# Feature maps and v copies of later batches tied behind named instructions, and the first load of q in two halves, in a linear-attention and Fourier-gate kernel on one core

## The chip, the cores and the metric

The kernel runs on one core of one Trainium2 chip. The metric is the device time of one execution in microseconds (us). Before the change three runs gave 295.21, 295.63 and 296.19 us; their median is 295.63 us. One more execution was profiled, and everything read from a trace here is that execution.

Engine names are those of the profile: PE is TensorE (matrix multiply; PEld its weight loads), DVE is VectorE, ACT is ScalarE, POOL is GpSimd, SP is SyncE. Each engine takes its instructions in the order in which they stand in its own program.

## The reference, cut to what matters

Eight batches, 8 heads, 576 positions, 64 values per head. Each batch goes through a linear attention with cosine and sine feature maps, and the result through a gated long convolution done with Fourier transforms.

```python
def phi(x, c, s):                      # feature map, 64 -> 128
    r = np.maximum(x, 0.0)
    return np.concatenate([r * c, r * s], axis=-1)
q_p = phi(q, cos_w, sin_w)
k_p = phi(k, cos_w, sin_w)
kv  = einsum('bhsf,bhsd->bhfd', k_p, v)
z   = k_p.sum(axis=2)
att = einsum('bhsf,bhfd->bhsd', q_p, kv) / (einsum('bhsf,bhf->bhs', q_p, z) + 1e-6)
x    = att as [batch, 576, 512]
x1, x2, x3 = split(x @ w_proj, 3)
conv = irfft(rfft(x2) * rfft(filter))  # along the 576 positions
out  = (x1 * conv * x3) @ w_out
```

## The kernel before, in words

Everything of one batch runs in a chain of stages, and stages of neighbouring batches are woven into each other.

**Stages of a batch.** `load_qk`, `load_v`: DMAs issued by POOL bring q, k and v in fp16 into tiles named qraw, kraw, vraw; all of them share one ring of four buffers (line 104, 109), so a load waits until the readers of the tile four loads earlier are done. `emit_phi`: twelve DVE multiplications per tensor make the feature maps qp and kp. `emit_va`: four ACT copies per batch (line 116) bring v into va, where a column of ones already stands. `emit_qt`: PE transposes qp in four pieces qt, and DVE and ACT each copy half of a piece to qpt. `emit_kv`: 48 matmuls of kp with va, one ACT cast to kvs. `emit_num`: matmuls of qpt with kvs, then on DVE rcp (the divisor) and att (the quotient), four pieces. `emit_fx`: att through a small first Fourier factor, ACT casts to fx. `emit_x2`: the x2 projection in three pieces, ACT casts to x2f. `emit_dft`: the forward transform, ACT casts to xf, DVE multiplies by the filter's spectrum h3 (m, yf). `emit_gate`: x1 and x3 projections, ACT cast to x1s, DVE product g. `emit_inv`: the inverse transform, ACT casts to eo, DVE sums to y. `emit_out`: y times w_out, ACT scales to os, SP's DMAs store it.

**Order.** The code at the end of the kernel (lines 619 to 709) emits the stages in a chosen sequence, but a scheduler decides where each instruction stands on its engine: as long as its operands are expected to be there in time, it may stand far ahead of where it was written. That is why, before the change, copies of v2 stand among batch 0's instructions on ACT.

**First part, batches 0 to 2 (to about 107 us).** Besides the stages, tables are computed here: POOL makes index rows (`emit_iotas`), DVE and ACT make sines and cosines. The inverse tables (`emit_inv_tables`) go DVE tn_inv, then two POOL instructions on tg_a (lines 245, 248), then ACT iim and ire. `emit_h` makes the spectrum: POOL forms feo, PE h_ps and h_nyq, ACT casts to h3 (lines 392, 399), DVE copies h3 once more.

**Later batches.** One turn of the loop at line 673 interleaves, for b from 1: x2(b) with num(b+1), dft(b), gate(b) with fx(b+1), inv(b), then out(b-1) with qt(b+2), then kv(b+2). A turn ends about where the first tile of out starts on PE.

**PSUM.** All matmul results use one pool of four tiles ("u", line 63). A new result waits until the readers of the tile whose place it takes are done. In a turn the places go: inv tiles 0 to 3; out_0 takes inv_0's place, qt_0 inv_1's, out_2 inv_2's, qt_1 inv_3's; out_4 takes out_0's (so it waits for the first os on ACT), qt_2 takes qt_0's, qt_3 takes out_2's (second os), kv takes qt_1's (its qpt copy on ACT), and the third x2 tile takes the place of the second num tile (its att on DVE).

Of the kernel before, what the change touches and what calls it, by code (L numbers as in the profile page):

```python
# [2 lines left out]

# [14 lines left out]
def kernel(  # L18
# [83 lines left out]
    def load_qk(b, nm):
        src = q if nm == "q" else k
        rw = work.tile([NP, NH, NJ * D], FP16, tag="raw", bufs=4, name=f"{nm}raw{b}")
        raw_t[(b, nm)] = rw
        nc.gpsimd.dma_start(out=rw, in_=src[b].rearrange("h (p j) d -> p h (j d)", j=NJ))
# [294 lines left out]

    kp_t, qp_t, kvs_t, att_t, fx_t, xt_t = {}, {}, {}, {}, {}, {}

    def emit_phi(b, nm):
# [3 lines left out]
        for j in range(NJ):  # L408
            for cs, col in ((0, ccol), (1, scol)):
                tsc(  # L410
                    t[:, j, :, cs], rw[:, :, ds(j * D, D)],
                    col[0:NP, j : j + 1], AL.mult, 0.0, AL.max,
                )
# [14 lines left out]
    def emit_qt(b, hp):  # L428
        qp, qpt = qp_t[b], qpt_buf[0]
        u = psum.tile([128, 2, 1024], FP16, tag="u", bufs=4, name=f"qt{b}_{hp}")  # L430
        for hh in range(2):
            for j in range(NJ):
                nc.tensor.transpose(  # L433
                    u[:, hh, ds(j * NP, NP)],
                    qp[:, j, 2 * hp + hh].rearrange("p a b -> p (a b)"),
                    perm,
                )
        hsl = slice(2 * hp, 2 * hp + 2)
        nc.vector.tensor_copy(  # L439
            out=qpt[:, hsl, :, 0, 0:60],  # L440
            in_=u[:, :, 0:300].rearrange("p h (t c) -> p h t c", c=60),
        )
        nc.scalar.copy(  # L443
            out=qpt[:, hsl, ::-1, 1, 4:64],
            in_=u[:, :, 276:576].rearrange("p h (t c) -> p h t c", c=60),
        )

    def emit_num(b, hp):
        qpt, kvs = qpt_buf[0], kvs_t[b]
        if hp == 0:  # L450
            att_t[b] = work.tile([128, NT, DM], FP16, tag="att", bufs=2, name=f"att{b}")
        att = att_t[b]
        u = unit(f"num{b}_{hp}")
        for hh in range(2):
            h = 2 * hp + hh
            for t in range(NT):
                nc.tensor.matmul(
                    u[:, hh, ds(t * 65, 65)], qpt[:, h, t].rearrange("p a b -> p (a b)"),
                    kvs[:, h // 4, ds((h % 4) * 65, 65)], start=True, stop=True,
                )  # L460
# [4 lines left out]
        nc.vector.tensor_tensor(  # L465
            out=att[:, :, ds(hp * 128, 128)].rearrange("p t (h d) -> p h t d", h=2),
            in0=nv[:, :, :, 0:D],
            in1=rcp.unsqueeze(3).to_broadcast([128, 2, NT, D]),
            op=AL.mult,
        )  # L470

    def emit_fx(b, cs=range(NC)):
        att = att_t[b]
        if 0 in cs:
            fx_t[b] = work.tile([128, NC, 24, 48], FP16, tag="fx", bufs=2, name=f"fx{b}")
        fx = fx_t[b]
        for c in cs:
            u = unit(f"fx{b}_{c}")
# [17 lines left out]
        nc.scalar.copy(  # L496
            out=fx[:, :, :, 40:48],
            in_=cu.rearrange("p u (c r) -> p (u c) r", c=2)[:, :, 0:192].rearrange(
                "p c (g o) -> p c g o", o=8
            ),  # L500
        )
# [4 lines left out]
    def emit_x2(b, bls=range(3)):  # L506
        fx = fx_t[b]
        if 0 in bls:
            moe.setdefault(b, {})["x2f"] = work.tile([NP, 3, 2, DM], FP16, tag="x2f", name=f"x2f{b}")
        x2f = moe[b]["x2f"]  # L510
        for bl in bls:
            u = unit(f"x2_{b}_{bl}")
            for comp in range(2):
                for c in range(NC):
                    nc.tensor.matmul(  # L515
                        u[0:NP, comp],
                        fx[:, c, ds(comp * 6 + 2 * bl, 2)].rearrange("p a b -> p (a b)"),
                        wp16[:, c, ds(DM, DM)], start=(c == 0), stop=(c == NC - 1),
                    )
            nc.scalar.mul(out=x2f[:, bl], in_=u[0:NP], mul=X2SC)  # L520

    def emit_dft(b):
        x2f = moe[b]["x2f"]
        yf = work.tile([NP, 3, 2, DM], FP16, tag="yf", name=f"yf{b}")
        moe[b]["yf"] = yf
        for bl in range(3):
            u = unit(f"dft{b}_{bl}")
            for comp, tab in ((0, tre), (1, tim)):
                nc.tensor.matmul(u[0:NP, comp], tab[:, bl], x2f[:, bl, comp], start=True, stop=True)  # L529
            xf = work.tile([NP, 2, DM], FP16, tag="xf", bufs=2, name=f"xf{b}_{bl}")  # L530
            nc.scalar.copy(out=xf, in_=u[0:NP])  # L531
            m1 = work.tile([NP, 2, DM], FP16, tag="m1", bufs=1, name=f"m1_{b}_{bl}")
            m2 = work.tile([NP, 2, DM], FP16, tag="m2", bufs=1, name=f"m2_{b}_{bl}")
            nc.vector.tensor_tensor(out=m1, in0=xf, in1=h3[:, bl, 1:3], op=AL.mult)  # L534
            nc.vector.tensor_tensor(
                out=m2, in0=xf, in1=h3[:, bl, 0].unsqueeze(1).to_broadcast([NP, 2, DM]), op=AL.mult
            )
            nc.vector.tensor_tensor(out=yf[:, bl, 0], in0=m1[:, 0], in1=m2[:, 1], op=AL.subtract)  # L538
            nc.vector.tensor_tensor(out=yf[:, bl, 1], in0=m1[:, 1], in1=m2[:, 0], op=AL.add)

    def emit_gate(b, c):
# [16 lines left out]
        nc.scalar.copy(out=x1s, in_=us[0][:, :, 0:HS])  # L558
        for hf in range(2):
            nc.vector.tensor_tensor(  # L560
                out=(g[:, c, 0:HS] if hf == 0 else g[:, c, HS:S][:, ::-1]).rearrange(
                    "p (j i o) -> p j i o", j=3, i=6
                ),
# [176 lines left out]
```

## Time and profile before

| what | value |
|---|---|
| three runs, median (lowest to highest) | 295.63 us (295.21 to 296.19) |
| the profiled execution's own time | 295.97 us |
| its span, first to last instruction | 294.2 us |
| mean granted TensorE clock | 0.949 |
| busy ACT, DVE, POOL | 198.5, 211.0, 40.2 us |
| issue of the first q load (576 KB) to its landing | 6.12 us |
| busy PE in 34 to 84 us, and in 107.1 to 136.7 us | 38.42 of 50 us, 28.86 of 29.6 us |

A line of the timeline reads: start and duration in us, engine, line of the code, operation, output<-input, shapes, how many were merged, and in square brackets how long the engine stood idle before it and what ended that wait. The chain of waits lists, in order of time, the pieces of work that follow from each other up to the last instruction.

### The profile page before, as it was taken

How to read it: one execution, taken by the hardware profiler on the slowest of the kernel's cores; microseconds unless marked ns; L12 is line 12 of the kernel's file. 1: busy time of each engine (PE TensorE's matmuls, PEld its weight loads, DVE VectorE, ACT ScalarE, POOL GpSimd, SP SyncE). 2: the span in 40 equal slices, each digit the busy share in tenths (PEclk: the TensorE clock that was granted, in tenths of full speed). 3: DMA queues.
4: the chain of work that ended last, by engine and by line, in shares of the span. 5: the costliest groups of instructions: out<-in, count | busy, mean ns of one | idle time of the engine just before them, and what ended most of it. 6: DMA issues, size and time to landing. Idle time of an engine off the chain costs nothing.

```text
span 294.2 us, 6029 instructions
## 1 busy us (share of the span) xinstructions
PE 255.1 (87%) x2379; PEld 179.8 (61%) x2379; DVE 211.0 (72%) x678; ACT 198.5 (67%) x266; POOL 40.2 (14%) x47
## 2 busy tenths in 40 slices
PE   0667883797899999899989998999999999999960
PEld 0554652744485867587758775877587768657620
DVE  4989498569699966996699669965796279508700
ACT  2186472969877779677967796776577767665531
POOL 8420839420102100300020000000000000000000
PEclk9999898579689999999999999999999999999995
DMA  7999889469235906690569050005000500050055
GB/s 95 204 205 207 139 125 196 60 89 178 21 63 78 166 2 163 88 156 0 164 84 159 1 163 2 0 3 163 0 0 2 162 1 2 0 160 3 1 162 160
DMA packets 26941, 26.67 MB, mean 91 GB/s; under 512 B 1632, under 2 KB 22112, under 8 KB 26912
## 3 DMA queue, kind: packets, MB, share of 16 engines
q0 software_dynamic: 21152, 16.84, 38.6%
q1 hardware_dynamic: 5760, 9.44, 11.6%
q8 instruction: 18, 0.29, 0.4%
q14 instruction: 11, 0.09, 0.1%
HBM read 33.69 MB, written 9.44 MB: 147 GB/s over the span
## 4 chain that ended last, share of the span: by engine, by line
PE 55%; DVE 17%; DMA 10%; ACT 7%; issue 4%; POOL 3%; SPq 1%; ACTq 0%; POOLq 0%; DVEq 0%
PE x L552 19%; PE out L601 9%; PE inv L578 9%; DMA vraw<-in_v_dram 7%; PE x L515 7%; DVE kp L90 7%; PE qt L433 5%; PE fx L480 3%; DVE qp L90 3%; DVE att L465 3%; ACT x2f L520 2%; POOL tg_a L245 2%; DMA qraw<-in_q_dram 2%; PE dft L529 1%; ACT va L116 1%
## 5 line engine op out<-in xcount | busy, mean ns | idle before, releaser
L552 PE MATMUL x<-fx,wp 128*128 128x288 f16 x512 | 69.0, 290 | 3.1 <-ACT fx L496 1.5
L552 PEld LDWEIGHTS <-wp 128*128 128x128 f16 x512 | 50.6, 99 | 17.7 <-issue 2.9
L515 PE MATMUL x<-wp,fx 128*96 128x512 f16 x192 | 45.1, 381 | 2.1 <-DVE att L465 1.7
L484 ACT CAST fx<-fx 128x960 f16<-128x960 f32 x32 | 30.3, 960 | 14.7 <-PE fx L480 14.6
L433 PE MATMUL qt<-perm,qp 96*128 96x96 f16 x384 | 24.2, 224 | 16.0 <-DVE qp L90 9.8
L520 ACT ACTIVATE x2f<-x 96x1024 f16<-96x1024 f32 x24 | 24.5, 1022 | 19.4 <-PE x L515 19.4
L116 ACT COPY va<-vraw 96x768 f16<-96x768 f16 x32 | 26.0, 836 | 16.9 <-DMA vraw<-in_v_dram 16.9
L601 PE MATMUL out<-wo,y 128*128 128x512 f16 x160 | 37.3, 379 | 0.0
L433 PEld LDWEIGHTS <-qp 96*128 96x128 f16 x384 | 21.8, 108 | 21.2 <-DVE qp L90 10.9
L560 DVE TENSOR_TENSOR g<-x,x1s 128x288 f16<-128x288 f32 x64 | 27.1, 447 | 9.3 <-PE x L552 5.0
L515 PEld LDWEIGHTS <-fx 128*96 128x96 f16 x192 | 22.2, 123 | 17.2 <-DVE att L465 2.5
L605 ACT ACTIVATE os<-out 128x1024 f32<-128x1024 f32 (+1 forms) x24 | 20.8, 882 | 15.7 <-PE out L601 10.9
L439 DVE COPY qpt<-qt 128x600 f16<-128x600 f16 x32 | 14.8, 467 | 17.0 <-PE qt L433 16.5
L465 DVE TENSOR_TENSOR att<-num,rcp 128x640 f16<-128x640 f32 x32 | 26.0, 819 | 0.2
L534 DVE TENSOR_TENSOR m<-xf,h 96x1024 f16<-96x1024 f16 x24 | 16.4, 682 | 13.4 <-ACT xf L531 13.2
L601 PEld LDWEIGHTS <-y 128*128 128x128 f16 x160 | 15.1, 98 | 15.3
L578 PEld LDWEIGHTS <-yf 96*128 96x128 f16 x192 | 19.3, 102 | 7.9 <-DVE yf L538 1.5
L531 ACT CAST xf<-dft 96x1024 f16<-96x1024 f32 x24 | 23.4, 1008 | 0.0
L558 ACT CAST x1s<-x 128x576 f16<-128x576 f32 x32 | 20.4, 639 | 3.9 <-PE x L552 1.7
L443 ACT COPY qpt<-qt 128x600 f16<-128x600 f16 x32 | 20.1, 659 | 3.5 <-DVE qpt L439 3.4
L582 ACT CAST eo<-inv 128x576 f16<-128x576 f32 x32 | 19.3, 657 | 3.1 <-PE inv L578 2.8
L480 PE MATMUL fx<-fm,att 128*128 128x240 f16 x128 | 18.9, 274 | 1.1 <-ACT fx L484 0.6
(152 smaller groups left out, 387.4 us busy)
## 6 DMA issues: line engine op xcount, KB each, us to landing
qraw<-in_q_dram POOLq DMA_DIRECT2D x8, 576.0 KB, 6.2
kraw<-in_k_dram POOLq DMA_DIRECT2D x8, 576.0 KB, 8.1
vraw<-in_v_dram POOLq DMA_DIRECT2D x8, 576.0 KB, 8.0
out_dram<-os SPq DMA_DIRECT2D x24, 192.0 KB, 2.5
out_dram<-os SPq DMA_DIRECT2D x24, 128.0 KB, 2.4
wp<-in_moe_w_proj_dram POOLq DMA_DIRECT2D x3, 512.0 KB, 12.0
out_dram<-os SPq DMA_DIRECT2D x24, 64.0 KB, 2.0
filt<-in_moe_filter_fft_dram POOLq DMA_DIRECT2D x2, 288.0 KB, 15.9
```

The costliest lines, as they stand in the source:

```text
L90: nc.vector.tensor_scalar(out=out, in0=in0, scalar1=s1, scalar2=s2, op0=op0, op1=op1)
L116: nc.scalar.copy(out=va_buf[b % 2][:, hs, :, 0:D], in_=raw_t[(b, "v")][:, hs].rearrange("p h (j d) -> p h j d", j=NJ),)
L433: nc.tensor.transpose(u[:, hh, ds(j * NP, NP)], qp[:, j, 2 * hp + hh].rearrange("p a b -> p (a b)"), perm,)
L465: nc.vector.tensor_tensor(out=att[:, :, ds(hp * 128, 128)].rearrange("p t (h d) -> p h t d", h=2), in0=nv[:, :, :, 0:D], in1=rcp.unsqueeze ...
L480: nc.tensor.matmul(u[:, t // 2, 0:480].rearrange("p (g o) -> p g o", o=20)[:, :, ds((t % 2) * 10, 10)], att[:, t, ds(c * 128, 128)], fm, s ...
L484: nc.scalar.copy(out=fx[:, c, :, 0:40].rearrange("p g (u o) -> p u g o", u=2), in_=u[:, :, 0:480].rearrange("p u (g o) -> p u g o", o=20),)
L515: nc.tensor.matmul(u[0:NP, comp], fx[:, c, ds(comp * 6 + 2 * bl, 2)].rearrange("p a b -> p (a b)"), wp16[:, c, ds(DM, DM)], start=(c == 0) ...
L520: nc.scalar.mul(out=x2f[:, bl], in_=u[0:NP], mul=X2SC)
L552: nc.tensor.matmul(u[:, hf, 0:HS], wp16[:, i, ds(w * DM + c * 128, 128)], fx[:, i, ds(12 + 6 * hf, 6)].rearrange("p a b -> p (a b)"), star ...
L560: nc.vector.tensor_tensor(out=(g[:, c, 0:HS] if hf == 0 else g[:, c, HS:S][:, ::-1]).rearrange("p (j i o) -> p j i o", j=3, i=6), in0=us[1 ...
L578: nc.tensor.matmul(u[:, comp, 0:HS], yf[:, bl, comp, ds(c * 128, 128)], tab[:, bl], start=(bl == 0), stop=(bl == 2),)
L601: nc.tensor.matmul(u[:, x], y[:, c, ds(OT[t], 128)], wo16[:, c], start=(c == 0), stop=(c == NC - 1),)
```

## The change

It does four things.

- The first load of q is issued as two loads of four heads each. Between them POOL makes three of the index rows; the load of k0 comes before the other rows. The feature map of q0 is computed in halves of four heads, so it is 24 DVE instructions of half the width in place of 12.
- The feature maps of later batches may not stand on DVE ahead of a chosen DVE instruction: qp1 behind the last att of batch 0, kp1 behind a g of gate 1 of batch 0, qp2 and kp2 behind the last qpt copy and the second att of batch 1, and in the loop q and k of batch n+1 behind the last qpt copy and the second att of batch n.
- The four copies of v may not stand on ACT ahead of a chosen ACT instruction: v1 behind the first x2f of batch 0, v2 behind the last fx cast (fxc) of batch 1, and in the loop v of batch n+1 behind fxc of batch n.
- This is done with `tc.issue_after(instruction)`, which adds an ordering edge within one engine and no semaphore.

```diff
+    def behind(*key):
+        return tc.issue_after(mark[key].ins) if key in mark else nullcontext()
...
-    load_qk(0, "q")
-    emit_iotas()
+    load_qk(0, "q", slice(0, 4))
+    emit_iotas(0)
+    load_qk(0, "q", slice(4, 8))
     load_qk(0, "k")
+    emit_iotas(1)
     load_v(0)
...
-    emit_phi(0, "q")
+    emit_phi(0, "q", 4)
...
-    emit_phi(1, "q")
+    with behind("att", 0, 3):
+        emit_phi(1, "q")
...
-    emit_phi(1, "k")
-    emit_va(1)
+    with behind("g", 0, 1):
+        emit_phi(1, "k")
+    with behind("x2f", 0, 0):
+        emit_va(1)
...
-    emit_phi(2, "q")
-    emit_phi(2, "k")
-    emit_va(2)
+    with behind("qpt", 1, 3):
+        emit_phi(2, "q")
+    with behind("att", 1, 1):
+        emit_phi(2, "k")
+    with behind("fxc", 1):
+        emit_va(2)
...
-            emit_phi(n + 1, "q")
-            emit_phi(n + 1, "k")
-            emit_va(n + 1)
+            with behind("qpt", n, 3):
+                emit_phi(n + 1, "q")
+            with behind("att", n, 1):
+                emit_phi(n + 1, "k")
+            with behind("fxc", n):
+                emit_va(n + 1)
```

Three places show what this does to the order. In the names the first number is the batch (va has two buffers, so va0 and va1 alternate), the last one only counts tiles.

ACT in the first part, before the change, from the last fx cast of batch 0 to the first qpt copy of batch 1:

```order
L496 CAST fx0_385<-fxc0_410 128x96x8
L116 COPY va1_84<-vraw1_116 96x12x64 x2
L558 CAST x1s0_0_448<-x0_0_0_430 128x576
L116 COPY va1_84<-vraw1_116 96x12x64 x2
...
L520 ACTIVATE x2f0_557<-x2_0_0_558 96x1024
L116 COPY va0_83<-vraw2_989 96x12x64
L520 ACTIVATE x2f0_557<-x2_0_1_568 96x1024
L116 COPY va0_83<-vraw2_989 96x12x64 x2
L520 ACTIVATE x2f0_557<-x2_0_2_578 96x1024
L443 COPY qpt0_82<-qt1_0_601 128x2x5x60
```

The same stretch of ACT after the change:

```order
L507 CAST fx0_398<-fxc0_423 128x96x8
L569 CAST x1s0_0_461<-x0_0_0_443 128x576
...
L531 ACTIVATE x2f0_570<-x2_0_0_571 96x1024
L124 COPY va1_84<-vraw1_117 96x12x64 x2
L531 ACTIVATE x2f0_570<-x2_0_1_581 96x1024
L124 COPY va1_84<-vraw1_117 96x12x64
L531 ACTIVATE x2f0_570<-x2_0_2_591 96x1024
L454 COPY qpt0_82<-qt1_0_614 128x2x5x60
```

The copies of v1 moved from ahead of x1s to behind the first x2f; the copies of v2 that stood between the x2f casts left this stretch altogether (all four now stand behind fxc1), and v3's left for the next turn.

ACT in a turn of the loop (b = 2), before, from the inverse transform's casts to kvs:

```order
L582 CAST eo2_1853<-inv2_3_1888 128x576
L605 ACTIVATE os1_1935<-out1_0_1936 128x1024
...
L443 COPY qpt0_82<-qt4_2_2001 128x2x5x60
L116 COPY va0_83<-vraw6_2853 96x12x64
L443 COPY qpt0_82<-qt4_3_2016 128x2x5x60
L116 COPY va0_83<-vraw6_2853 96x12x64
L425 CAST kvs4_2080<-kv4_2031 128x520
L116 COPY va0_83<-vraw6_2853 96x12x64
L520 ACTIVATE x2f3_2082<-x2_3_0_2083 96x1024
```

The same stretch after the change:

```order
L593 CAST eo2_1866<-inv2_1_1879 128x576
L124 COPY va0_83<-vraw4_1916 96x12x64
L593 CAST eo2_1866<-inv2_2_1890 128x576
L593 CAST eo2_1866<-inv2_3_1901 128x576
L124 COPY va0_83<-vraw4_1916 96x12x64 x3
L616 ACTIVATE os1_1948<-out1_0_1949 128x1024
...
L454 COPY qpt0_82<-qt4_3_2029 128x2x5x60
L436 CAST kvs4_2093<-kv4_2044 128x520
L531 ACTIVATE x2f3_2095<-x2_3_0_2096 96x1024
```

The four copies moved from around kvs to the casts of the inverse transform, three of them in one block ahead of the first os; and the batch that they serve is 4 where it was 6. There are five such blocks, for v3 to v7.

DVE in the same turn: between the last qpt copy and the first rcp there stood, for num of batch 3, six multiplications of qp5 and nine of kp4. The last rows of these, before:

```order
L90 TENSOR_SCALAR kp4_1918<-kraw4_1901,scol_68 96x8x64
L90 TENSOR_SCALAR kp4_1918<-kraw4_1901,ccol_67 96x8x64
L88 TENSOR_SCALAR rcp3_0_1630<-num3_0_1619 128x10
L90 TENSOR_SCALAR kp4_1918<-kraw4_1901,scol_68 96x8x64
L464 RECIPROCAL rcp3_0_1630<-rcp3_0_1630 128x10
```

After, the twelve of qp4 stand there and none of kp4; the end of them:

```order
L90 TENSOR_SCALAR qp4_1918<-qraw4_1912,ccol_67 96x8x64
L90 TENSOR_SCALAR qp4_1918<-qraw4_1912,scol_68 96x8x64
L88 TENSOR_SCALAR rcp3_0_1643<-num3_0_1632 128x10
L475 RECIPROCAL rcp3_0_1643<-rcp3_0_1643 128x10
L88 TENSOR_SCALAR rcp3_1_1658<-num3_1_1647 128x10
```

So the first rcp has twelve multiplications ahead of it where it had fifteen; kp4 follows between and behind the att instructions, one more stands between m and yf of the forward transform, and two ahead of the last g.

More of the change, by code (lines that the diff above doesn't have):

```diff
@@ L2 @@
 import math
-from contextlib import ExitStack
+from contextlib import ExitStack, nullcontext
 import concourse.bass as bass
@@ L97, with load_qk @@
     cc = {}
+    mark = {}
+    def behind(*key):
+        return tc.issue_after(mark[key].ins) if key in mark else nullcontext()
     raw_t = {}
[L102 removed]
+    def load_qk(b, nm, hs=slice(0, NH)):
         src = q if nm == "q" else k
[L104 to L106 removed]
+        if hs.start == 0:
+            rw = work.tile([NP, NH, NJ * D], FP16, tag="raw", bufs=4, name=f"{nm}raw{b}")
+            raw_t[(b, nm)] = rw
+        nc.gpsimd.dma_start(
+            out=raw_t[(b, nm)][:, hs], in_=src[b, hs].rearrange("h (p j) d -> p h (j d)", j=NJ)
+        )
     def load_v(b):
@@ L407, in emit_phi @@
         (kp_t if nm == "k" else qp_t)[b] = t
[L408 to L413, printed above, removed]
+        for h0 in range(0, NH, nh):
+            for j in range(NJ):
+                for cs, col in ((0, ccol), (1, scol)):
+                    tsc(
+                        t[:, j, h0 : h0 + nh, cs], rw[:, h0 : h0 + nh, ds(j * D, D)],
+                        col[0:NP, j : j + 1], AL.mult, 0.0, AL.max,
+                    )
     def emit_kv(b):
@@ L438, in emit_qt @@
         hsl = slice(2 * hp, 2 * hp + 2)
-        nc.vector.tensor_copy(
+        mark["qpt", b, hp] = nc.vector.tensor_copy(
             out=qpt[:, hsl, :, 0, 0:60],
@@ L464, in emit_num @@
         nc.vector.reciprocal(out=rcp, in_=rcp)
-        nc.vector.tensor_tensor(
+        mark["att", b, hp] = nc.vector.tensor_tensor(
             out=att[:, :, ds(hp * 128, 128)].rearrange("p t (h d) -> p h t d", h=2),
@@ L495, in emit_fx @@
             )
-        nc.scalar.copy(
+        mark["fxc", b] = nc.scalar.copy(
             out=fx[:, :, :, 40:48],
@@ L519, in emit_x2 @@
                     )
-            nc.scalar.mul(out=x2f[:, bl], in_=u[0:NP], mul=X2SC)
+            mark["x2f", b, bl] = nc.scalar.mul(out=x2f[:, bl], in_=u[0:NP], mul=X2SC)
     def emit_dft(b):
@@ L530, in emit_dft @@
             xf = work.tile([NP, 2, DM], FP16, tag="xf", bufs=2, name=f"xf{b}_{bl}")
-            nc.scalar.copy(out=xf, in_=u[0:NP])
+            mark["xf", b, bl] = nc.scalar.copy(out=xf, in_=u[0:NP])
             m1 = work.tile([NP, 2, DM], FP16, tag="m1", bufs=1, name=f"m1_{b}_{bl}")
@@ L557, in emit_gate @@
         x1s = work.tile([128, 2, HS], FP16, tag="x1s", bufs=2, name=f"x1s{b}_{c}")
-        nc.scalar.copy(out=x1s, in_=us[0][:, :, 0:HS])
+        mark["x1s", b, c] = nc.scalar.copy(out=x1s, in_=us[0][:, :, 0:HS])
         for hf in range(2):
-            nc.vector.tensor_tensor(
+            mark["g", b, c] = nc.vector.tensor_tensor(
                 out=(g[:, c, 0:HS] if hf == 0 else g[:, c, HS:S][:, ::-1]).rearrange(
```

12 lines of the change are left out of this document (7 added, 5 removed).

## The prediction

> **What bounds the kernel now.** I read the page first, then the chain of waits, then the timeline engine by engine.
>
> ```profile
> span 294.2 us, 6029 instructions
> PE 55%; DVE 17%; DMA 10%; ACT 7%; issue 4%; POOL 3%; SPq 1%; ACTq 0%; POOLq 0%; DVEq 0%
> ```
>
> PE holds only 55% of the chain. The chain in order of time shows where it does:
>
> ```profile
> 1.28 6.12 DMA qraw<-in_q_dram
> ...
> 17.97 15.28 DMA vraw<-in_v_dram
> ...
> 61.49 6.13 DMA vraw<-in_v_dram
> ...
> 107.07 1.73 PE out L601 x8
> ...
> 136.69 1.73 PE out L601 x8
> ...
> 195.95 1.73 PE out L601 x8
> ...
> 225.15 1.73 PE out L601 x8
> ...
> 231.52 1.53 PE kv L420 x48
> ...
> 253.95 4.32 PE out L601 x20
> ```
>
> Two loads of v stand in the first part, 21.4 us together. From 107.07 on the first out tiles mark the turns: 29.62 us, twice 29.63, then 29.20 and 28.80. The last turn has no v copies and no feature maps left and is PE without gaps but one; so 28.80 is PE's floor, and turns lose 0.82, 0.83, 0.83 and 0.40 us. The first 107 us hold the time to be won. On ACT they look so:
>
> ```profile
> 33.27 1.57 ACT L116 COPY va<-vraw 96x768 f16<-96x768 f16 x2 [4.65 <-DMA vraw<-in_v_dram]
> ...
> 42.50 1.02 ACT L520 ACTIVATE x2f<-x 96x1024 f16<-96x1024 f32 x1 [0.54 <-PE x L515]
> 49.99 0.83 ACT L116 COPY va<-vraw 96x768 f16<-96x768 f16 x1 [6.47 <-DMA vraw<-in_v_dram]
> ...
> 54.01 2.47 ACT L443 COPY qpt<-qt 128x600 f16<-128x600 f16 x4
> 56.38 0.92 ACT L254 ACTIVATE iim<-tg_a 96x864 f16<-96x864 f32 x1
> 57.96 0.59 ACT L425 CAST kvs<-kv 128x520 f16<-128x520 f32 x1 [0.66 <-PE kv L420]
> ...
> 59.60 1.00 ACT L256 ACTIVATE ire<-tg_a,half_pi 96x864 f16<-96x864 f32 x1
> ...
> 64.76 1.93 ACT L392 ACTIVATE h<-h_ps 96x1024 f16<-96x1024 f32 x2
> ...
> 81.37 0.64 ACT L582 CAST eo<-inv 128x576 f16<-128x576 f32 x1 [0.56 <-PE inv L578]
> ```
>
> ACT stands 4.65 us for v1 and 6.47 us for v2 with x1s and x2f queued behind; PE then stands because its PSUM places aren't read out.
>
> **The change part by part.** Times are of the profiled span; "was" is before, "is" my value after.
>
> *First q in halves.*
>
> ```profile
> 7.50 0.67 DVE L90 TENSOR_SCALAR qp<-qraw,scol 96x512 f16<-96x512 f16 x1 [2.16 <-DMA qraw<-in_q_dram]
> ...
> 12.25 0.34 DVE L90 TENSOR_SCALAR kp<-kraw,ccol 96x512 f16<-96x512 f16 x1
> 12.51 0.34 DVE L90 TENSOR_SCALAR kp<-kraw,scol 96x512 f16<-96x512 f16 x1
> ...
> 13.17 2.15 DVE L439 COPY qpt<-qt 128x600 f16<-128x600 f16 x4
> ...
> 17.34 0.34 DVE L90 TENSOR_SCALAR kp<-kraw,scol 96x512 f16<-96x512 f16 x1
> ```
>
> The whole load took 6.12 us from 1.28. No row has half of it; it can't land before half of that (4.34) nor after the whole (7.40). I take the middle, 5.9, and DVE idles 2.16 us there anyway. qp0 with the small instructions between took 7.50 to 12.25, 4.75 us; twelve more instructions of half width I put at 0.45 more, so qp0 ends at 11.1. The qpt copies ended at 15.3, 3.1 us after qp0, since PE had most transposes still to do; with heads 0 to 3 transposed beforehand I estimate 1.8, 12.9. Then kp0, now all twelve, at 0.26 each (12.25 to 12.51): 16.0, was 17.68. **Gain 1.7 us**; 0 if the half lands with the whole and the copies wait as before, 3.2 at the other end. It passes on, for the matmuls of kv wait on the last kp.
>
> *v1 and v2 off ACT's way.*
>
> ```profile
> 28.68 5.60 PE L552 MATMUL x<-fx,wp 128*128 128x288 f16 x31 [1.50 <-ACT fx L496]
> ...
> 35.41 0.82 DVE L560 TENSOR_TENSOR g<-x,x1s 128x288 f16<-128x288 f32 x2 [4.23 <-ACT x1s L558]
> ...
> 44.45 1.11 DVE L90 TENSOR_SCALAR tn_inv<-srow,fc 96x288 f32<-96x288 f32 x3
> ```
>
> Gate 0 started on PE at 28.68, is 27.0. A g needs two tiles of eight matmuls, 16 x 0.18 = 2.9, and latency: 30.3, was 35.41. The DVE instructions from there to the end of tn_inv are nearly the same (10.2 us), so tn_inv ends at 40.5, was 45.6. **Gain 5.1 here.** On ACT the x2f of piece 0, 42.50 before, is about 38.5 (5 us by DVE's shift, less 1 for PE, which now has 64 matmuls and 8 of x2 to do from 27.0). v1 landed at 33.27; its copies now come at 39.5 and find it. Then two copies (1.57), x2f, a copy (0.83), x2f, the qpt copies with the last va (2.47 + 0.8): ACT reaches iim at 47.0, was 56.38. But iim waits for POOL:
>
> ```profile
> 45.65 6.16 POOL L245 TENSOR_SCALAR tg_a<-tn_inv 96x864 f32<-96x864 f32 x1 [0.47 <-DVE tn_inv L90]
> 51.90 2.01 POOL L248 TENSOR_TENSOR tg_a<-tg_a,tn_inv 96x864 f32<-96x864 f32 x1
> ```
>
> 40.5 plus 0.1, 6.16 and 2.01, with gaps: 48.9. So the next wait is POOL's, and 1.9 us of ACT's gain stay there. From iim to the end of ire took 56.38 to 60.60, less 0.66 idle: 3.6, then three h casts of 1.0: h3 is done at 55.6, was 66.69. **Gain 11.1.**
>
> That needs PE to have the spectrum's matmuls ready:
>
> ```profile
> 51.79 1.12 PE L433 MATMUL qt<-perm,qp 96*128 96x96 f16 x12 [4.85 <-ACT x2f L520]
> ...
> 57.73 1.50 PE L388 MATMUL h_ps<-filt,hs__666 96*96 96x512 f16 x3
> ...
> 62.82 0.81 PE L388 MATMUL h_ps<-feo,hs__666 96*96 96x512 f16 x3
> ...
> 81.13 3.21 PE L433 MATMUL qt<-perm,qp 96*128 96x96 f16 x48
> 84.17 1.69 PE L420 MATMUL kv<-va,kp 96*128 96x65 f16 x48
> ```
> ```profile
> 54.00:57.00 3.00, 2.84 (x47) 2.84 (x47) 1.74 (x7) 2.95 (x6) 0.83 (x1) 0.50 0.30 24
> ```
>
> kv1 waits for the last copy of v1 and ends at 46.9; 24 matmuls follow. Before, after 4.85 us idle, the granted clock was 0.50 (third number from the end) and three took 1.50 us; later 0.81. At 0.27 each they are done at 53.4, in time for h3; at 0.5 at 59. I take the fast ones, since no gap on PE in my walk there is above 2 us.
>
> From h3 to the last eo took 66.69 to 82.01, 15.3 us, with four va copies in it; after, also four (v2's behind fxc). So 70.9. Then 48 transposes still stood on PE, and kv2 began 2.2 us later; now twelve are left, 1.0 us: 71.9, was 84.17, **gain 12.3**. kv2 to the first out took 22.9 us, 0.5 over the 22.4 of the last full turn (231.52 to 253.95); I take 0.4 of it as gone: first out at 94.4, **gain 12.7**.
>
> *The turns.*
>
> ```profile
> 120.31 1.93 PE L515 MATMUL x<-wp,fx 128*96 128x512 f16 x8 [0.50 <-DVE att L465]
> ...
> 135.00 2.37 ACT L582 CAST eo<-inv 128x576 f16<-128x576 f32 x4
> ...
> 138.46 1.02 ACT L605 ACTIVATE os<-out 128x1024 f32<-128x1024 f32 x1 [1.09 <-PE out L601]
> ...
> 141.01 1.03 PE L601 MATMUL out<-wo,y 128*128 128x512 f16 x4
> ```
>
> The third x2 tile waits for att, and that for the 15 multiplications ahead; three fewer at 0.26 are 0.79 us: this wait goes, and with kvs clear of va copies the turn's 0.8. New: three va copies ahead of os, one among the eo. An eo adds 0.57 (four in 2.37), a copy 0.74 (two in 1.57): os starts at 135.00 + 4 x 0.57 + 4 x 0.74 = 140.24, was 138.46, and ends 141.26. PE's out_4, at 141.01, waits for it: 0.3; qt_3 and kv wait for the second os and its qpt copy: 0.3 more. The cover was the 1.5 us from os's end (139.48) to out_4. So a turn is 28.80 + 0.6 = 29.4, five times 147.0; before, 107.07 to 253.95 was 146.88. **Sum of the turns: +0.1**; between -2.9 (the copies cost nothing) and +4 (old waits stay too). The kp moved behind att fill 0.26 and 0.52 us where DVE waited 0.87 for PE ahead of the last g, or before m: nothing. Loads: q, k and v of a batch are issued most of a turn ahead, and v1 and v2 no longer have a reader waiting.
>
> **Sum.** -12.7 + 0.1 = -12.6; the span 281.6. The profiled execution took 295.97, 1.77 more than its span: 283.4. The median is 0.34 below 295.97, which I leave inside the range.
>
> **The rivals.**
>
> *POOL is quicker* (0.15). Its first tg_a took three times the second's 2.01, beside ten qp2 multiplications on DVE; after the change these stand behind qpt, and DVE mostly waits then. If POOL is done by 47.0, 1.9 us more are won: 281.5. For it speaks the place, against it that the two are different operations.
>
> The Trainium skill, "SBUF — State Buffer", section "Who interferes with whom", says that DVE's two-port instructions, tensor_scalar among them, and GpSimd exclude each other for a whole instruction. By that rule this case holds; the row of 6.16 agrees, but shows no tensor_scalar alone. The sum would be 281.5 by the rule, 283.4 by the row.
>
> *TensorE stays at half clock* (0.12) after the small gaps on PE: the spectrum's matmuls end at 58.9, a cast of 1.0 behind them puts h3 at 59.9, 4.3 later: 287.7. The row at 0.50 speaks for it, the missing long gap against.
>
> *The block of copies falls on PE whole* (slower, 0.05). If os, out_4 and kv had no slack, each of five blocks would cost 4 x 0.74 = 2.96, 14.8 us: 295.97 - 12.7 + 14.8 = 298.1. It decides from 2.5 us a block; the 1.5 us between os and out_4 speak against it.
>
> *The copies still wait* (0.03): were v1 more than 6 us late, ACT would stand at 39.5 as it stood at 33: about 295.6.
>
> **How the numbers follow.** My forecast, 283.4, has 0.65: from 281.5 to 287, by the first load (0 to 3.2) and the turns. The range 280.5 to 288 takes in the first two rivals and half of the turns' lower bound; outside lie the slower case, the one without effect and the forecast's tails, under 0.2. What differs by under 0.3% (0.9 us) a measurement can't tell from no change. Faster 0.92, same 0.03, slower 0.05.
>
> **What would show it.** In the changed profile: no idle of ACT for vraw, or under 1 us; POOL's first tg_a at 40 to 41; h3 done near 55.6; first out near 94.4; turns of 29.4, with a wait of PE's out_4 on os. Wrong it would be if ACT or PE waited elsewhere before 70 us, or if turns passed 30 us.

## The result and the profile after

The changed kernel takes **284.56 us** (median; 284.35 to 284.68), the kernel before 295.81 us (295.21 to 296.19, now four runs) on the same chip: ratio 0.962, 95% interval 0.960 to 0.964. Forecast were 283.4 us, range 280.5 to 288.0. So the sign, the size and the range held. Several terms of the sum did not (the halves, gate 0, POOL, the transposes of batch 2, the turns), and their errors partly cancelled, which is luck. What each kind of pin contributes was told incompletely, which only the experiments show.

The first lines of the page, and its group of the copies of v (busy us, mean ns; then ACT's idle us just before them); the last line is the same group before the change:

```profile
span 282.7 us, 6035 instructions
...
PE 70%; DVE 11%; ACT 10%; issue 3%; POOL 2%; SPq 1%; DMA 1%; ACTq 0%; POOLq 0%; DVEq 0%
...
L124 ACT COPY va<-vraw 96x768 f16<-96x768 f16 x32 | 25.2, 854 | 0.0
```
```profile
L116 ACT COPY va<-vraw 96x768 f16<-96x768 f16 x32 | 26.0, 836 | 16.9 <-DMA vraw<-in_v_dram 16.9
```

PE now holds 70% of the chain (was 55), DMA 1% (was 10), and ACT has no idle time ahead of a va copy. The chain of waits in order of time has no load of v left; its first out tiles mark the turns (start, us, what):

```profile
97.45 1.73 PE out L612 x8
...
126.52 1.73 PE out L612 x8
...
155.59 1.73 PE out L612 x8
...
184.66 1.73 PE out L612 x8
...
213.74 1.73 PE out L612 x8
...
242.81 4.32 PE out L612 x20
```

First out 9.62 us earlier (was 107.07); five turns of 29.07 us, 145.36 in all (were 146.88); the rest of the span, from 242.81 to its end, 39.9 us (was 40.25). So the 11.5 us of the span are 9.6 + 1.5 + 0.4.

How the 9.6 came about is read from the timelines of DVE and POOL where gate 0 stands (start, us, engine, line, op; idle time before and what ended it in brackets):

```profile
31.92 0.82 DVE L571 TENSOR_TENSOR g<-x,x1s 128x288 f16<-128x288 f32 x2 [1.51 <-PE x L563]
32.66 2.79 DVE L261 SCALAR_TENSOR_TENSOR tg_a<-tg_a,tn_h 96x864 f32<-96x864 f32 x1
35.38 3.19 DVE L88 TENSOR_SCALAR t<-t 1x288 f32<-1x288 f32 x1
38.50 0.80 DVE L571 TENSOR_TENSOR g<-x,x1s 128x288 f16<-128x288 f32 x2
...
44.67 0.91 DVE L90 TENSOR_SCALAR tn_inv<-srow,fc 96x288 f32<-96x288 f32 x3
```
```profile
31.46 6.95 POOL L386 TENSOR_TENSOR feo<-filt 96x1536 f16<-96x1536 f16 x2 [12.49 <-DMA filt<-in_moe_filter_fft_dram]
...
45.99 3.13 POOL L255 TENSOR_SCALAR tg_a<-tn_inv 96x864 f32<-96x864 f32 x1
49.20 2.01 POOL L258 TENSOR_TENSOR tg_a<-tg_a,tn_inv 96x864 f32<-96x864 f32 x1
```

The first g starts 3.5 us earlier than before, and the next one no earlier at all (38.50; before 38.28): between them DVE stands in a tg_a of 2.79 us and in a t of one partition and 288 elements, 3.19 us, for as long as POOL's two feo run. The same t instruction before the change, at 45.96, took 0.29 us. So tn_inv ends at 45.58, before at 45.56: by the end of gate 0 nothing was won. Then ACT finds v1 landed, no copy of v2 stands between the x2f casts any more, and POOL's first tg_a takes 3.13 instead of 6.16 us:

```profile
42.27 1.02 ACT L531 ACTIVATE x2f<-x 96x1024 f16<-96x1024 f32 x1 [2.24 <-PE x L526]
43.20 1.55 ACT L124 COPY va<-vraw 96x768 f16<-96x768 f16 x2
...
51.24 0.92 ACT L264 ACTIVATE iim<-tg_a 96x864 f16<-96x864 f32 x1 [0.98 <-POOL tg_a L258]
...
55.60 1.90 ACT L402 ACTIVATE h<-h_ps 96x1024 f16<-96x1024 f32 x2
```

iim starts at 51.24 (was 56.38), h3 is done at 57.5 (was 66.69). Of the 4.1 us between these two gains, 3.1 come from PE: before, ACT waited 0.66 us for kv and, at 63.02, 2.42 us for h_ps, whose groups of three matmuls started 1.29 us apart at a granted clock of 0.50; after, they start 0.65 us apart at 1.00, and neither wait is there. Another 0.7 us is a copy of v2 that stood between the h casts at 64.03.

### The profile page after: what moved, and what is told of

The parts are those of the page before. It is cut to its first block, busy times and chain, and to the rows that moved or that the text cites. A ratio compares the mean times of both kernels' runs of the same rounds, so it can differ in the third digit from the quotient of the medians.

```text
span 282.7 us, 6035 instructions
## 1 busy us (share of the span) xinstructions
PE 249.5 (88%) x2379; PEld 176.7 (63%) x2379; DVE 218.8 (77%) x690; ACT 196.2 (69%) x266; POOL 37.9 (13%) x48
## 4 chain that ended last, share of the span: by engine, by line
PE 70%; DVE 11%; ACT 10%; issue 3%; POOL 2%; SPq 1%; DMA 1%; ACTq 0%; POOLq 0%; DVEq 0%
PE x L563 21%; PE x L526 13%; PE out L612 10%; PE inv L589 7%; PE fx L491 4%; PE kv L431 4%; PE qt L444 4%; PE num L468 3%; DVE kp L90 3%; ACT x2f L531 3%; ACT fx L495 2%; PE dft L540 2%; DVE qp L90 2%; SPq L626 1%; POOL tg_a L255 1%
## 5 line engine op out<-in xcount | busy, mean ns | idle before, releaser
L495 ACT CAST fx<-fx 128x960 f16<-128x960 f32 x32 | 30.3, 961 | 14.6 <-PE fx L491 14.5
L444 PE MATMUL qt<-perm,qp 96*128 96x96 f16 x384 | 23.3, 216 | 8.2 <-DVE qp L90 8.0
L444 PEld LDWEIGHTS <-qp 96*128 96x128 f16 x384 | 20.5, 103 | 13.8 <-DVE qp L90 9.3
L124 ACT COPY va<-vraw 96x768 f16<-96x768 f16 x32 | 25.2, 854 | 0.0
L612 PEld LDWEIGHTS <-y 128*128 128x128 f16 x160 | 15.3, 98 | 15.7
L90 DVE TENSOR_SCALAR qp<-qraw,scol 96x512 f16<-96x512 f16 (+1 forms) x54 | 20.8, 386 | 0.0
## 6 DMA issues: line engine op xcount, KB each, us to landing
qraw<-in_q_dram POOLq DMA_DIRECT2D x2, 288.0 KB, 5.1
```

What stands on the lines that cost most here:

```text
L90: nc.vector.tensor_scalar(out=out, in0=in0, scalar1=s1, scalar2=s2, op0=op0, op1=op1)
L124: nc.scalar.copy(out=va_buf[b % 2][:, hs, :, 0:D], in_=raw_t[(b, "v")][:, hs].rearrange("p h (j d) -> p h j d", j=NJ),)
L444: nc.tensor.transpose(u[:, hh, ds(j * NP, NP)], qp[:, j, 2 * hp + hh].rearrange("p a b -> p (a b)"), perm,)
L495: nc.scalar.copy(out=fx[:, c, :, 0:40].rearrange("p g (u o) -> p u g o", u=2), in_=u[:, :, 0:480].rearrange("p u (g o) -> p u g o", o=20),)
L612: nc.tensor.matmul(u[:, x], y[:, c, ds(OT[t], 128)], wo16[:, c], start=(c == 0), stop=(c == NC - 1),)
```

## The experiments

Each run was taken beside runs of the kernel before on the same chip. The table puts together what the accounts below rest on: the start of the first out in the chain and the sum of the five turns, both of the one execution that was profiled, and the median time of all executions (for e2 and e10 the chain has no row at the first out; there it is the timeline's start plus 0.16, the distance of the two views in the others). The ratios go by the runs of before on the same chip, whose medians were 295.2 to 295.8.

| kernel | differs from after by | first out | five turns | time, us | ratio to before [95%] |
|---|---|---|---|---|---|
| before | all | 107.07 | 146.88 | 295.8 | |
| after | | 97.45 | 145.36 | 284.6 | 0.962 [0.960, 0.964] |
| e1 | no q and k pins, no halves | 105.24 | 148.11 | 295.1 | 1.000 [0.998, 1.001] |
| e2 | no v pins, no halves | 111.87 | 161.82 | 314.9 | 1.067 [1.063, 1.070] |
| e3 | no halves | 97.06 | 145.36 | 285.0 | 0.965 [0.963, 0.966] |
| e4 | feo on DVE | 97.88 | 145.36 | 284.7 | 0.962 [0.957, 0.967] |
| e5 | no pins in the loop | 107.70 | 146.87 | 294.6 | 0.997 [0.995, 0.999] |
| e6 | no pins of batches 1 and 2 | 109.17 | 145.32 | 296.8 | 1.004 [1.002, 1.007] |
| e7 | no q pin in the loop | 105.69 | 145.32 | 293.3 | 0.993 [0.990, 0.995] |
| e8 | a faster version, first try | 97.28 | 145.31 | 283.4 | 0.960 [0.957, 0.962] |
| e9 | no k pin in the loop | 97.85 | 148.83 | 288.4 | 0.975 [0.973, 0.977] |
| e10 | no v pin in the loop | 102.28 | 159.54 | 304.1 | 1.028 [1.026, 1.030] |
| e11 | a faster version, second try | 94.04 | 145.33 | 281.3 | 0.949 [0.946, 0.952] |
| e12 | nothing (after once more) | 97.25 | 145.36 | 284.3 | 0.963 [0.960, 0.965] |

**Only the pins of v (e1).** The pins of q of batch 2 and all pins of k go likewise, and the first load of q is whole.

```
-    with behind("att", 0, 3):
-        emit_phi(1, "q")
+    emit_phi(1, "q")
...
-            with behind("qpt", n, 3):
-                emit_phi(n + 1, "q")
+            emit_phi(n + 1, "q")
```

> Only the copies of v are pinned (batches 1, 2 and those of the loop); the feature maps keep the places of before and the first load of q is whole. Theory A (the v pins carry nearly all; the feature maps count through POOL only): the first part loses against after 0.7 us by the whole load and 2 to 3 us by the twelve qp2 multiplications that stand beside POOL's first tg_a again (6.2 us instead of 3.1), and the turns up to 0.8 each where x2 waits for att: 287 to 291 us. Rival B (v pins alone): no loss but the load's 0.7, 285.3 us. Rival C (both are needed): ACT is free, but DVE's order holds PE as before, above 292 us.

Measured: 295.1 us, no difference from before. Theory A was wrong by 4 us and B by 10; C holds. DVE shows where the wait went:

```profile
46.12 0.33 DVE L90 TENSOR_SCALAR qp<-qraw,scol 96x512 f16<-96x512 f16 x1
...
61.01 0.35 DVE L90 TENSOR_SCALAR qp<-qraw,ccol 96x512 f16<-96x512 f16 x1 [3.18 <-DMA qraw<-in_q_dram]
```

ACT has no wait for v after 15 us any more, but the qp of the batch after next now stand in DVE's order ahead of the h copies and att, and wait 3.18 us for q; and POOL's first tg_a is back at 6.34 us, beside qp multiplications like the one at 46.12.

**Only the pins of q and k (e2).** The mirror image; the v pins of batches 2 and later go likewise, and the first load of q is whole.

```
-    with behind("x2f", 0, 0):
-        emit_va(1)
+    emit_va(1)
```

> Only the feature maps are pinned; the copies of v keep the places that the order gives them without a pin, and the first load of q is whole. Theory A: ACT stands for v1 and v2 again (about 11 us idle for vraw in the group of va copies), first out later than 104 us, turns about 29.1 to 29.4: 293 to 296 us. Rival B: the same. Rival C (the feature maps carry it): below 290 us.

Measured: 314.9 us, far outside all of them. ACT's idle time ahead of the copies, 16.9 us before, has grown:

```profile
L124 ACT COPY va<-vraw 96x768 f16<-96x768 f16 x32 | 25.7, 835 | 32.7 <-DMA vraw<-in_v_dram 32.7
```

Now ACT waits in the turns too. The four raw tiles are shared by q, k and v. What POOL's issue of v waits for stands in the views of all waits (us in total, times, longest), of after and then of e2:

```profile
POOL vraw L119 <- DVE kp L90: 66.0, 6, 14.8
```
```profile
POOL vraw L119 <- DVE rcp L88: 51.7, 3, 17.3
```

In after the load of v takes over a raw tile that a kp frees. In e2 the three long waits (17.2 to 17.3 us each) end with the first rcp instructions behind the twelve pinned qp (the last qp starts at 121.55, the next rcp at 121.86, and v is issued at 122.67). So I read it that there a qp frees the tile: pinned late, it makes v late, and a copy of v that isn't pinned too then stands on ACT. The waits are in the views; which instruction frees the tile is inferred from the order.

**No halves (e3).**

```
-    load_qk(0, "q", slice(0, 4))
+    load_qk(0, "q")
...
-    emit_phi(0, "q", 4)
+    emit_phi(0, "q")
```

> After with the first load of q whole and its feature map in twelve full-width multiplications; all pins stay. Theory A: the 0.66 us that kv main starts earlier passes on to the end: 285.2 us, 0.7 slower than after. Rival: feo and with it gate 0 hang on the landing of filt, which the second issue of q delays by about 1 us, so that the halves bring nothing or cost: 284.0 to 284.6 us.

Measured: 285.0 us. The time doesn't decide: it lies at theory A's 285.2 and above the rival's range, but its ratio can't be told from after's (0.965 [0.963, 0.966] against 0.962 [0.960, 0.964]). The execution that was profiled is also the fastest of the four (284.14 us; the others 284.92 to 285.08). Its trace shows the rival's mechanism:

```profile
30.53 7.20 POOL L386 TENSOR_TENSOR feo<-filt 96x1536 f16<-96x1536 f16 x2 [11.01 <-DMA filt<-in_moe_filter_fft_dram]
...
37.68 0.87 POOL L112 DMA_DIRECT2D qraw<-in_q_dram  x1
```

filt lands 0.93 us earlier than with the halves, feo ends 0.7 us earlier (38.4 in after), and it is feo's end from which gate 0 goes on. In this execution the 0.66 us won at kv main are lost there: tn_inv ends at 44.80 without the halves, and at 45.58 and 44.73 with them (after and e12). What the halves are worth in time stays open: the medians are 0.4 us apart, the ratios 0.3%.

**feo on DVE (e4).**

```
-            nc.gpsimd.tensor_tensor(
+            nc.vector.tensor_tensor(
                 out=feo[:, x].rearrange("p j n -> p (j n)"), ...
```

> After with the two feo additions on DVE instead of POOL; everything else stays, though the order of DVE shifts around them. Theory A (POOL's feo keeps DVE's tg_a of 2.79 and the 1x288 t of 3.19 us from running in gate 0): both come down to below 1.2 us together, feo costs DVE 2 to 3.4 us instead, and tn_inv ends 1.5 to 3 us earlier: 281.5 to 283.5 us. Rival (the long rows are waits of another kind, for data or for ACT, put down to the instruction): they stay long, and DVE only gets more work: 285 to 288 us.

Measured: 284.69 us, as after, but one of four executions 281.65 us. DVE (first fence) is as theory A says, PE (second) is not what it counted on:

```profile
31.60 0.95 DVE L386 TENSOR_TENSOR feo<-filt 96x1536 f16<-96x1536 f16 x1 [1.62 <-DMA filt<-in_moe_filter_fft_dram]
```
```profile
44.69 0.67 PE L444 MATMUL qt<-perm,qp 96*128 96x96 f16 x12 [0.97 <-ACT x2f L531]
45.72 1.30 PE L431 MATMUL kv<-va,kp 96*128 96x65 f16 x36 [0.35 <-ACT qpt L454]
47.56 0.82 PE L431 MATMUL kv<-va,kp 96*128 96x65 f16 x12 [0.54 <-ACT va L124]
48.19 1.50 PE L398 MATMUL h_ps<-filt,hs__679 96*96 96x512 f16 x3
```
```profile
44.00:48.00 4.00, 2.42 (x57) 0.89 0.99 142
48.00:52.00 4.00, 4.00 (x16) 0.50 0.55 67
```

feo takes 0.95 us on DVE instead of 3.5 on POOL, the tg_a 1.04 instead of 2.79, the t 0.97 instead of 3.19, and tn_inv ends at 42.6, 2.9 us earlier; iim starts at 48.29. So the long rows of after were DVE shut out by POOL. One thing else differed: from 28 to 32 us the granted clock was 1.00 here and 0.57 in after. It isn't the cause of the short rows: in e3 it was 1.00 too, with tg_a at 2.87 and t at 3.19 us, and in e8, with feo on DVE, it was 0.59, with tg_a at 1.04 us and tn_inv done at 42.8. But PE, idle for 0.97, 0.35 and 0.54 us between 43.7 and 47.6 and busy for 2.42 of 4 us (windows: length, busy, granted clock, DMA), fell to a granted clock of 0.50, and h3 was done at 57.4, where it was before. The Trainium skill, "SBUF — State Buffer", section "Who interferes with whom", says that DVE instructions in a two-port mode, which tensor_scalar can take, and GpSimd exclude each other for a whole instruction, and that a DVE instruction with two SBUF inputs, as tg_a has here, contends with a GpSimd instruction that reads SBUF. These two runs agree with it: 3.19 and 2.79 us beside feo, 0.97 and 1.04 away from it.

**No pins in the loop (e5), and none outside it (e6).** e5 (first piece, and so for k and v) and e6 (second piece, and so for k of batch 1 and for batch 2):

```
-            with behind("qpt", n, 3):
-                emit_phi(n + 1, "q")
+            emit_phi(n + 1, "q")
...
-    with behind("att", 0, 3):
-        emit_phi(1, "q")
+    emit_phi(1, "q")
```

> The pins of batches 1 and 2 stay, all three pins inside the loop (batches 3 to 7) go. Theory A2 (a pin only helps if no other engine takes over the wait for the same late load: without the loop's pins the qp of batch 3 stand in DVE's order ahead of the h copies and wait there for q's load near 58 to 61 us): h3 is done 2 to 4 us later than in after, first out 99 to 102 us, the turns 29.6 each as in before; 289 to 293 us. Rival D (what the first part wins is decided by the first part's pins): first out 97.5 us, only the turns go back, 5 x 0.55 = 2.8 us: 287.4 us.

> The loop's pins stay, those of batches 1 and 2 go; the halves of q stay. Theory A2: ACT stands for v1 and v2 again, about 10 us, first out 104 to 107 us; the turns 29.1: 291 to 294 us. Rival D: the same within 1 us; what differs is whether this and the run without the loop's pins add up: by A2 their two losses against after sum to more than the 10.7 us between after and before, by D to just that.

Measured: 294.6 and 296.8 us. Against after, 10.0 and 12.2 us are lost, 22 in all, where after is worth 11. So the two do not add up, and rival D falls; A2 has the direction right and both sizes too small (first out 107.7 and 109.2, not 99 to 102 and 104 to 107). The turns do add up: without the loop's pins they are before's to 0.01 us, with them after's to 0.04. In e6 ACT waits for v 3.9 us only, not 10; the larger wait is DVE's, for q of batch 1, with att of batch 0 behind it:

```profile
26.12 0.35 DVE L90 TENSOR_SCALAR qp<-qraw,ccol 96x512 f16<-96x512 f16 x1 [6.02 <-DMA qraw<-in_q_dram]
```

**No q pin in the loop (e7).** One pin of nine is taken away.

```
-            with behind("qpt", n, 3):
-                emit_phi(n + 1, "q")
+            emit_phi(n + 1, "q")
```

> After without the loop's pin of qp alone; kp and v keep theirs. Theory A2: this one pin carries the loss of the run without any loop pin in the first part: DVE waits 2 to 3.5 us for q of batch 3 near 58 us, first out 99 to 101 us; in the turns 0.2 to 0.8 each: 287 to 291 us. Rival D: first out 97.5 us and the turns within 0.2 of 29.07: 284.6 to 285.6 us.

Measured: 293.3 us; the turns are after's, but the first out is 8.2 us late. A2's mechanism holds, its sizes do not (99 to 101 us, 0.2 to 0.8 a turn, 287 to 291 us in all). DVE and then PE:

```profile
56.62 0.35 DVE L90 TENSOR_SCALAR qp<-qraw,ccol 96x512 f16<-96x512 f16 x1 [3.26 <-DMA qraw<-in_q_dram]
...
83.11 0.35 DVE L90 TENSOR_SCALAR qp<-qraw,ccol 96x512 f16<-96x512 f16 x1 [3.83 <-DMA qraw<-in_q_dram]
```
```profile
61.18 0.66 PE L540 MATMUL dft<-x2f,tre 96*96 96x512 f16 x1 [2.04 <-DVE att L476]
...
78.01 2.67 PE L431 MATMUL kv<-va,kp 96*128 96x65 f16 x48 [1.87 <-ACT qpt L454]
...
88.00 3.24 PE L526 MATMUL x<-wp,fx 128*96 128x512 f16 x8 [0.57 <-DVE att L476]
```

The two waits sum to 7.1 us. The first makes the dft 2.1 us late (59.07 in after) and kv of batch 2 3.1 (74.86); behind the second, the last x2 of batch 1 starts 6.9 us late (81.09 in after) and runs at a lower clock, 3.24 instead of 1.91 us. That makes 8.2.

**No k pin in the loop (e9).**

```
-            with behind("att", n, 1):
-                emit_phi(n + 1, "k")
+            emit_phi(n + 1, "k")
```

> After without the loop's pin of kp alone (qp and v keep theirs). Theory A3 (a pin is worth something only where the order puts a reader of a load ahead of the landing; the order without this pin still leaves the kp of batch 3 behind the att of batch 2): first part as in after, first out 97 to 98 us, the kp stand ahead of att or g in the turns without waiting for k's load: 284.3 to 286 us. Rival A2 strict (each of the three pins is needed, or DVE takes the wait over): DVE waits over 2 us for a k load and the total is above 288 us.

Measured: 288.4 us, and neither theory: the total is the rival's, but no kp waits for a load. The first out is after's within 0.4 us, and four of the turns are 29.85 to 29.97:

```profile
108.89 0.47 DVE L90 TENSOR_SCALAR kp<-kraw,scol 96x512 f16<-96x512 f16 x1
109.50 0.82 DVE L476 TENSOR_TENSOR att<-num,rcp 128x640 f16<-128x640 f32 x1
110.36 0.29 DVE L90 TENSOR_SCALAR kp<-kraw,ccol 96x512 f16<-96x512 f16 x1
110.57 0.81 DVE L476 TENSOR_TENSOR att<-num,rcp 128x640 f16<-128x640 f32 x1
```
```profile
111.44 1.93 PE L526 MATMUL x<-wp,fx 128*96 128x512 f16 x8 [0.57 <-DVE att L476]
```

Five kp (108.02 to 110.36) stand ahead of the att that x2 waits for, at 110.57, and x2 waits again: 0.9 us in a turn.

**No v pin in the loop (e10).**

```
-            with behind("fxc", n):
-                emit_va(n + 1)
+            emit_va(n + 1)
```

> After without the loop's pin of v alone (qp and kp keep theirs, and v1 and v2 too). Theory A3: the order puts the first copies of batch 3 behind the first qpt copy of batch 2, near 75 us, and those of later batches among x1s and fx; ACT waits 1.5 to 4 us for v in each, PE with it: turns 31 to 34 us, first out 98 to 101: 293 to 308 us. Rival D: the copies find v landed, since it is issued most of a turn ahead: 284.5 to 287 us.

Measured: 304.1 us. A3 holds, with the first out (102.28) a little later than its 98 to 101: three turns of 34.2, 34.0 and 33.7 us, and ACT waits up to 3.7 us for v:

```profile
119.05 1.56 ACT L124 COPY va<-vraw 96x768 f16<-96x768 f16 x2 [3.72 <-DMA vraw<-in_v_dram]
```

**A faster version (e8, e11).** e8 takes e4 and changes three places (the third pin holds all instructions of t0 and t1):

```
-        with behind("x2f", 0, 0):
+        with behind("x2f", 0, 2):
             emit_va(1)
...
-    emit_kv(1)
     emit_h()
+    emit_kv(1)
...
-        tsc(t0, srow[0:1], 0.25, AL.mult)
+        with behind("qpt", 1, 3):
+            tsc(t0, srow[0:1], 0.25, AL.mult)
...
```

> A version meant to be faster than after: feo on DVE as before in its run, the copies of v of batch 1 behind the third x2f, the three t instructions behind the last qpt copy of batch 1, and the matmuls of kv of batch 1 written after those of h, so that PE has no gap of 0.5 us or more between 42 and 56 us. Theory E (in the run with feo on DVE the 3 us that DVE, POOL and ACT won were lost to TensorE's clock of 0.50 after gaps on PE of 0.24 to 0.97 us): the clock stays at 1.00 from 44 to 56 us, h3 is done at 54 us or earlier, first out 94.5 to 96: 281.5 to 283 us. Rival F (the gain is lost further on, at att, fx or kv of batch 2, whatever the clock): first out 97 to 98: 284 to 285 us.

Measured: 283.35 us, first out 97.28: the first out is F's, the time lies between the two (the profiled execution, 284.31 us, is the slowest of four). PE kept a granted clock of 1.00 from 32 to 52 us, and h3 was done at 51.8. Then the gain was lost in a way that neither had:

```profile
54.73 2.05 PE L469 MATMUL num<-kvs,qpt 128*128 128x65 f16 x40 [1.83 <-ACT kvs L437]
```
```profile
46.41 5.89 POOL L258 TENSOR_TENSOR tg_a<-tg_a,tn_inv 96x864 f32<-96x864 f32 x1
```

kvs stood behind h, iim and tg_a on ACT, PE waited 1.83 us for it, and ran at a clock of 0.68 from 56 to 60 us. (POOL's second tg_a, 2.01 us in after, took 5.89 beside the qp of DVE: the same exclusion, the other way round.) e11 adds three pins, the last on the y multiplications of batch 0, taken out of emit_inv:

```
+        with behind("kvs", 1) if pool else nullcontext():
             nc.scalar.activation(out=sin_dst, in_=a, func=AF.Sin, scale=TWO_PI)
...
-    with behind("att", 1, 1):
+    with behind("yf", 0):
         emit_phi(2, "k")
...
+    for c in range(NC):
+        with behind("qpt", 2, 3):
+            emit_y(0, c)
```

> The faster version again, with three more edits in the first part: the activations of iim and ire stand behind the kvs cast of batch 1, the kp of batch 2 behind the last yf of batch 0, and the y multiplications of batch 0 behind the last qpt copy of batch 2. Theory E (what is left after 50 us is DVE and ACT work that stands ahead of kvs and qpt without being needed yet, and PE's half clock behind those gaps): num of batch 1 starts at 53.5 to 54 us instead of 54.7, kv of batch 2 at 70 to 72.5 us instead of 74, first out 93 to 95.5 us, span 278 to 281: 280 to 283 us. Rival G (TensorE's clock gives it back whatever the order): first out above 96.5 us: 283 to 284.5 us.

> After itself, unchanged, on the same chip as the runs above, so that the faster version is compared with it and not only with before: 284 to 285 us.

Measured on one chip: e11 **281.27 us**, ratio to before 0.949 [0.946, 0.952]; after 284.31 us, 0.963 [0.960, 0.965]. The intervals lie apart: e11 is 1.1% faster than after. The first out stands where E puts it:

```profile
94.04 1.73 PE out L619 x8
...
123.11 1.73 PE out L619 x8
```
```profile
53.24 1.39 PE L470 MATMUL num<-kvs,qpt 128*128 128x65 f16 x40 [0.68 <-ACT kvs L438]
...
70.78 1.69 PE L433 MATMUL kv<-va,kp 96*128 96x65 f16 x48 [0.33 <-ACT qpt L456]
```

num starts at 53.24 (56.16 in after), kv of batch 2 at 70.78 (74.86), the turns are still 29.07.

## Why the prediction was right or wrong

| step | predicted | measured |
|---|---|---|
| kv of batch 0, by the halves | 1.7 earlier | 0.66 earlier; gone by tn_inv (e3) |
| gate 0 starts on PE; its first g | 27.0; 30.3 | 28.02; 31.92 |
| tn_inv done | 40.5 | 45.58 (before 45.56) |
| ACT at iim | 48.9 | 51.24 |
| h3 done | 55.6 | 57.5 |
| kv of batch 2 | 71.9 | 74.86 |
| first out | 94.4, gain 12.7 | 97.45, gain 9.6 |
| five turns | +0.1 | -1.5 |
| span | 281.6 | 282.7 |

*The halves.* The mechanism is there, the size was off. The half had landed by 5.64, but the half-width multiplications follow each other at 0.195 us against 0.26 for the whole, so twelve more of them and the small instructions took until 11.84, not 11.1; kp0 ended at 17.02, not 16.0. That it "passes on, for the matmuls of kv wait on the last kp" was wrong beyond gate 0: the trace of e3 shows gate 0's end hanging on filt and feo.

*Gate 0.* This is the step that failed: "The DVE instructions from there to the end of tn_inv are nearly the same (10.2 us)". They are the same instructions, but they took 13.7 us, since they stood beside another POOL. Of the 5.1 us that tn_inv is later than forecast, 3.5 are this; 1.0 is gate 0's later start, and 0.6 its first g, whose 16 matmuls took 3.8 us at a granted clock of 0.57, not 2.9. The timelines of before, DVE and POOL:

```profile
36.15 1.94 DVE L251 SCALAR_TENSOR_TENSOR tg_a<-tg_a,tn_h 96x864 f32<-96x864 f32 x1
```
```profile
30.42 6.75 POOL L376 TENSOR_TENSOR feo<-filt 96x1536 f16<-96x1536 f16 x2 [10.88 <-DMA filt<-in_moe_filter_fft_dram]
```

There tg_a began one us ahead of feo's end, 37.17, and what followed ran free. Moved forward, tg_a and t fall beside feo and are shut out: 2.79 and 3.19 us. e4 is the evidence: with feo away from POOL, 2.9 us come back against after (2.1 against e12, where gate 0 had full clock as in e4). The other trace of after, e12, shows the same from another side. There the first g started at 30.43, tg_a came just ahead of feo (31.47) and ran free, and t and hb were shut out in its place (hb took 0.44 us in after):

```profile
31.16 1.04 DVE L261 SCALAR_TENSOR_TENSOR tg_a<-tg_a,tn_h 96x864 f32<-96x864 f32 x1
32.13 3.19 DVE L88 TENSOR_SCALAR t<-t 1x288 f32<-1x288 f32 x1
...
35.98 2.75 DVE L373 TENSOR_TENSOR hb<-hs__679,sgn 96x288 f16<-96x288 f16 x1
```

So tn_inv ended at 44.73 there, still 4.2 us later than forecast. I had weighed the exclusion for POOL's tg_a alone and not for its feo, whose row stood in the same timeline.

*POOL quicker.* This rival came true, 3.13 instead of 6.16 us. By luck it gave back some 3 of the 5 us that gate 0 missed, and so iim was only 2.3 us later than forecast.

*TensorE.* Full clock in the matmuls of h, as forecast. The rival of the half clock did not happen there in after; it did in e4. Both were priced too high: the rows of three matmuls (0.81 and 1.50 us) overlap and start 0.65 and 1.29 us apart, so 24 matmuls take 5.2 or 10.3 us, not 6.5 or 12.

*The transposes.* From h3 to the last eo took 15.1 us, as forecast (15.3). But all 48 transposes of batch 2 still stood behind it on PE (from 71.75), not the twelve forecast, so kv of batch 2 began 2.2 us after the last eo, as before, and not 1.0. With h3 1.9 us late, that makes its 3.0.

*The turns.* The old waits went (0.8 us each; e9 puts the kp pin's part at 0.9 in four of five turns, the prediction had 0.79). The block of three va copies ahead of os cost 0.27 us (29.07 against the floor of 28.80), not 0.6: in the first turn os ended at 101.87, and out_4 started on PE 4.63 us after out_0 (97.28 to 101.91), before 4.49 (106.90 to 111.39), so it waited some 0.14 us. So the term was mis-sized by 0.33 us a turn, 1.6 in all. The 3.1 us missing before the first out and these 1.6 stand against each other; that the total is closer than its parts is luck.

*Which part does it.* The prediction followed the order of after and so held all pins at once, but gave the reason to the copies of v ("v1 and v2 off ACT's way") and none to the loop's qp: "q, k and v of a batch are issued most of a turn ahead". e1 shows that the v pins alone are worth nothing, e2 that the others alone cost nearly 20 us, e7 that without one q pin 8.2 of the 9.6 us are gone. The load is late because its raw tile comes free late; the pins take away the readers that stand in an engine's queue ahead of work that PE needs. As long as one of q or v is left there (e1, e2, e5, e6, e7, e10), the wait only changes the engine. The kp of the loop (e9) waited for no load; their pin is worth the time of the kp themselves.

What stays open: how small a gap on PE lowers the granted clock. e4's fell after gaps of up to 0.97 us; that of e11 stood at 1.00 from 52 to 60 us through gaps of up to 0.68 and fell later. In after it was 0.50 from 29 to 31 us behind a gap of 1.50; in e12, the same kernel, it was 1.00 there behind one of 1.42. No run varied one gap alone.

## What to carry to other kernels

When instructions of an in-order engine wait for late loads, look for every reader of every load that shares the same buffers, on all engines, and move all of them behind what is needed first; here, with one kind alone moved, the wait went to the next engine or the next load. When a wait is taken away, look what then runs at the same time: here DVE work slid beside POOL's feo and lost there what it had won. And give the term of an overlap its price from the other engine's row too, even where the operation is as small as one partition.

## What the runs showed of the hardware

- A DVE tensor_scalar on 1x288 elements took 3.19 us beside POOL's addition of 96x1536 (after and e12), 0.29 us without it (before). A tensor_tensor of 96x288 with both inputs in SBUF (hb) took 2.75 us beside it (e12), 0.44 without (after). The g (tensor_tensor that reads PSUM) at 31.92 took its usual 0.82 us beside the same addition.
- The addition of 96x1536 in fp16 took 0.95 us on DVE (e4) and 3.1 to 3.7 us on POOL (two in 6.21 to 7.45 us, with DVE at work beside it).
- The clock of TensorE fell to 0.50 where PE was busy for 2.42 of 4 us and no single gap in the 5 us before reached 1 us (e4).
